# A three-stage attention and MLP kernel: first head pair in an older form, four subtractions on another engine, last accumulator in two halves

## The chip, the cores and the metric

The kernel runs on one core of a Trainium2 chip. The metric is device time in microseconds (us) of one execution. Five engines of the core work side by side and wait for each other through semaphores: PE (TensorE, the matrix unit; PEld is its weight load), DVE (VectorE), ACT (ScalarE), POOL (GpSimd) and SP (SyncE, which here only issues DMAs). Each takes its instructions strictly in the order in which the program wrote them, so an instruction that waits holds up all that stand behind it on that engine.

## The reference

Inputs and outputs are float32. Clustered attention over 2 batches, 8 heads, 768 positions and 64 features (16 clusters per head), then two MLPs over 1536 tokens (512 to 2048 to 512):

```python
q_assign = argmax(q/|q| @ (centroids/|centroids|).T)      # k_assign likewise
scores = (q @ k.T) / 8, -1e9 where q_assign != k_assign
x = softmax(scores) @ v                                   # heads side by side: 1536 x 512
h = x @ moe_w_in;  x = (h * cos(h)) @ moe_w_out
h = x @ moe2_w_in; x = where(h > 0, h, exp(min(h, 0)) - 1) @ moe2_w_out
```

## The kernel before

Every product is made from high and low halves of its float32 operands (a rounded copy and the rest), in three matmuls that add into one accumulator. So each operand costs an engine two instructions: a copy (the high half) and a subtraction (the low half).

**Attention.** The 16 heads form 8 pairs (pp = 0 to 7). A pair is prepared (loads of `nat_k`, `nat_q`, `nat_v`; transposes; high and low halves; norms; similarity to the centroids; cluster masks) while the pair ahead of it runs through its 12 steps `qk`, `rowmax`, `expo`, `turn`, `p_hi`, `p_lo`, with `av` behind every third. Pairs 1 to 7 write their halves to tiles `hi` and `lo` and spread them into the operand stacks `X0k, X1k, T0k, T1k` (and q) by six DMAs per tensor (`stack`, L755 to L760). The first pair has a path of its own without those DMAs: `first_pe` transposes each head, `first_hi`, `first_low` and `first_hi2` write the stacks from PSUM, and its two heads are normed, compared and masked one after the other, with nothing on PE to hide behind. In this kernel its Newton steps for the norms, those of the centroids too (`cen_step`, keys `c`), are POOL instructions (`norm_step`, L656 to L662); low half `X1q` goes to POOL through an extra copy `fraw` (`first_raw`); and squares of its second head are folded once on POOL before DVE sums them (L832).

**MLPs.** Each has three token tiles t of 512 and 16 slices f of 128 hidden columns. Tile t = 0 runs `g1` (12 matmuls into h), `act` (the activation, then its halves `GH` on the engine that table `OWN` names and `GL`) and `g2` (12 matmuls into four accumulators) per slice, while `w_part` rebuilds the weights of that slice from their loaded form (L163, L165, L167), and splits them (high half `slot`, low half L175). Tiles 1 and 2 take the slices in pairs p = 0 to 7 with seven half-sized products per pair (`prod`, L480), `post`, and `act2`, whose last step is the subtraction `GL` at L544, for every pair on POOL. Weights of the second MLP take the places of the first's as its last tile frees them (`load_w`).

**What sets the order.** Tables of numbers (`FIRST`, `PAIR`, `STEP`, `HALF`, `UNIT`, `LAST`, `MLP`, `WINO`, `WB`) give each step a time; the program sorts all steps by it and writes them in that order, which is then the order on every engine and of SP's queue. `OWN` and the `_ON` tables name engines. The last accumulators are copied by ACT (`finish`, L561) and stored through SP (L565).

Of the kernel before, what the change touches and what calls it, by code (L numbers as in the profile page):

```python
# [8 lines left out]
F32 = mybir.dt.float32  # L9
# [6 lines left out]
ALU = mybir.AluOpType  # L16
# [1304 lines left out]
```

## Time and profile before

| | us |
|---|---|
| three timed runs: median (lowest to highest) | 789.33 (786.51 to 790.74) |
| the profiled execution, its own time | 789.13 |
| its span | 787.3 |
| busy in the span: PE / DVE / ACT / POOL | 766.7 / 612.9 / 553.8 / 402.3 |
| first scores matmul of the attention | 19.85 after the span's start |
| boundary of the MLPs (first `g1` of the second) | 518.57 |
| last matmul starts | 783.14 |

The table is read against the first line: 1.83 us of the profiled execution lie outside its span. PE is busy in 97% of the span, so time is found in the few stretches in which it idles or runs at the lower of its two clock levels.

### The profile page before, as it was taken

The numbers are of one execution on the slowest core, as the hardware profiler recorded it, in microseconds if no ns is written. First come the engines' busy times: TensorE is split into PE (matmuls) and PEld (weight loads), VectorE is DVE, ScalarE is ACT, GpSimd is POOL, SyncE is SP. The second block draws the span as 40 slices with busy tenths as digits, with TensorE's granted clock in tenths as the row PEclk, the third lists the DMA queues.
The fourth block names the chain that finished last, engine by engine and source line by source line (L and its number), as shares of the span: only waits on it lengthen the run. The fifth ranks groups of instructions, "written<-read, shape, count | busy, mean of one in ns | idle before, by whom it ended". The sixth has DMA issues, their size and how long they took to land.

```text
span 787.3 us, 13051 instructions
## 1 busy us (share of the span) xinstructions
PE 766.7 (97%) x4579; PEld 686.5 (87%) x4579; DVE 612.9 (78%) x1008; ACT 553.8 (70%) x1035; POOL 402.3 (51%) x472
## 2 busy tenths in 40 slices
PE   6899999999999999999999999989999999999998
PEld 5789999999998878889999899968888999999996
DVE  6789899898899989989998844688978577663442
ACT  5788988989989988867666755766755554654343
POOL 7755866866865732444655422251228666532221
PEclk9899999999999999999999999999999999999999
DMA  5546657647437395011123238882000222223221
GB/s 122 121 98 154 147 117 161 138 104 182 101 87 267 39 374 210 1 40 61 62 81 121 71 113 285 292 275 102 0 1 25 110 81 82 81 95 120 81 80 54
DMA packets 72145, 93.27 MB, mean 118 GB/s; under 512 B 31440, under 2 KB 52432, under 8 KB 72080
## 3 DMA queue, kind: packets, MB, share of 16 engines
q1 hardware_dynamic: 71936, 92.41, 39.4%
q8 instruction: 36, 0.59, 0.3%
q14 instruction: 29, 0.24, 0.1%
q10 hardware_dynamic: 144, 0.03, 0.0%
HBM read 58.75 MB, written 15.78 MB: 95 GB/s over the span
## 4 chain that ended last, share of the span: by engine, by line
PE 91%; ACT 3%; POOL 2%; DVE 1%; DMA 1%; issue 1%; SPq 1%; ACTq 0%; POOLq 0%
PE a L280 32%; PE h L480 20%; PE h L221 11%; PE px L1093 8%; PE pt L1062 8%; PE s L1039 4%; PE s L1042 4%; PE pt_sim L874 2%; PE pt_raw L718 1%; ACT P L1053 1%; POOL GL L544 1%; ACT PH L1076 1%; DMA nat_q<-in_q_dram 1%; DMA X1k<-lo 1%; SPq L607 0%
## 5 line engine op out<-in xcount | busy, mean ns | idle before, releaser
L544 POOL TENSOR_TENSOR GL<-A,GH 128x512 fp32r<-128x512 f32 x64 | 93.3, 1463 | 155.2 <-ACT GH L93 118.4
L280 PE MATMUL a<-GH,slot 128*128 128x512 f32 x384 | 124.7, 393 | 0.0
L280 PE MATMUL a<-slot,GH 128*128 128x512 f32 x384 | 118.4, 389 | 0.0
L1082 DVE TENSOR_TENSOR PL<-pt,PH 128x384 fp32r<-128x384 f32 x192 | 99.0, 547 | 16.5 <-ACT PH L1076 16.5
L1076 ACT ACTIVATE PH<-pt 128x384 fp32r<-128x384 f32 x192 | 85.0, 496 | 18.5 <-PE pt L1062 18.3
L1047 DVE TENSOR_REDUCE m<-s 128x1 f32<-128x768 f32 x96 | 91.0, 948 | 4.2 <-PE s L1042 3.5
L1053 ACT ACTIVATE P<-s,m 128x768 f32<-128x768 f32 x96 | 87.3, 910 | 0.9 <-DVE m L1047 0.6
L280 PEld LDWEIGHTS a<-GH,slot 128*128 128x128 f32 x384 | 72.7, 189 | 14.8
L1062 PE MATMUL pt<-ident,P 128*128 128x128 f32 x576 | 84.2, 280 | 0.0
L221 PE MATMUL h<-XH,slot 128*128 128x512 f32 x256 | 83.7, 391 | 0.0
L280 PEld LDWEIGHTS a<-slot,GH 128*128 128x128 f32 x384 | 71.0, 188 | 14.0
L480 PE MATMUL h<-XH,slot 128*128 128x256 f32 x384 | 81.8, 282 | 0.0
L280 PE MATMUL a<-GL,slot 128*128 128x512 f32 x192 | 75.6, 394 | 3.7 <-POOL GL L544 3.7
L280 PE MATMUL a<-slot,GL 128*128 128x512 f32 x192 | 74.8, 389 | 0.0
L1062 PEld LDWEIGHTS pt<-ident,P 128*128 128x128 f32 x576 | 67.3, 142 | 6.3 <-DVE PL L1082 1.2
L93 ACT ACTIVATE GH<-A 128x512 fp32r<-128x512 f32 x86 | 53.9, 627 | 21.2 <-DVE A L539 9.3
L391 POOL TENSOR_TENSOR X<-slot 128x512 f32<-128x512 f32 x32 | 49.0, 1543 | 37.0 <-DVE sums L434 23.5
L480 PEld LDWEIGHTS h<-XH,slot 128*128 128x128 f32 x384 | 65.0, 190 | 0.7
L502 DVE TENSOR_TENSOR X<-X 128x256 f32<-128x256 f32 x32 | 23.4, 733 | 49.1 <-ACT X L500 48.9
L1093 PE MATMUL px<-PL,V 128*128 128x384 f32 x192 | 57.9, 356 | 0.7
L1093 PE MATMUL px<-PH,V 128*128 128x384 f32 x192 | 58.2, 357 | 0.0
L221 PEld LDWEIGHTS h<-XH,slot 128*128 128x128 f32 x256 | 48.2, 189 | 10.3 <-DVE slot L175 0.3
(197 smaller groups left out, 1958.6 us busy)
## 6 DMA issues: line engine op xcount, KB each, us to landing
raw<-in_moe_w_in_dram SPq DMA_DIRECT2D x32, 512.0 KB, 7.9
raw<-in_moe_w_out_dram SPq DMA_DIRECT2D x32, 512.0 KB, 8.8
sd<-sums SPq DMA_DIRECT2D x32, 384.0 KB, 2.3
sums<-sd SPq DMA_DIRECT2D x32, 384.0 KB, 3.5
nat_k<-in_k_dram SPq DMA_DIRECT2D x16, 192.0 KB, 3.3
nat_q<-in_q_dram SPq DMA_DIRECT2D x16, 192.0 KB, 3.8
nat_v<-in_v_dram SPq DMA_DIRECT2D x8, 384.0 KB, 4.4
xr<-row SPq DMA_DIRECT2D x32, 96.0 KB, 3.5
```

Source lines behind the costliest of these rows:

```text
L93: nc.scalar.activation(out=out, in_=in_, func=AF.Copy)
L221: nc.tensor.matmul(h, lhsT=a[:, kd, :], rhs=b, start=(kd == 0 and i == 0), stop=(kd == NKD - 1 and i == 2))
L280: nc.tensor.matmul(accs[m, t][e], lhsT=a, rhs=b, start=(f == 0 and i == 0), stop=(f == NF - 1 and i == 2))
L391: eng.tensor_tensor(out=u[:, i].rearrange("p e n -> p (e n)").rearrange("p (k f) -> p k f", k=NKD), in0=f32(ih), in1=f32(il), op=ALU.add)
L480: nc.tensor.matmul(o, lhsT=x[:, k], rhs=piece(y, k), start=(k == 0 and n == 0), stop=(k == 1 and n == 2))
L544: eng.tensor_tensor(out=GL, in0=A, in1=f32(GH), op=ALU.subtract)
L1047: nc.vector.tensor_reduce(out=m, in_=st[n]["s"][:, :, 0:HW], axis=AX.XY, op=ALU.max, negate=True)
L1053: nc.scalar.activation(out=P, in_=st[n]["s"][:, :, 0:HW], func=AF.Exp, bias=st[n]["m"], accum_out=den_all[:, u % NDEN, j, r, 0:1])
L1062: nc.tensor.transpose(pt[:, c * 128:(c + 1) * 128], st[n]["P"][:, e, c * 128:(c + 1) * 128], ident)
L1076: nc.scalar.activation(out=ph, in_=pt, func=AF.Copy)
L1082: nc.vector.tensor_tensor(out=pl, in0=pt, in1=f32(ph), op=ALU.subtract)
L1093: nc.tensor.matmul(tx[g][:, 0:HW], lhsT=V2s[pp][:, j, c, :], rhs=halves[g][a][:, c, :], start=(n == 0), stop=(n == 2 * C - 1))
```

## The change

The path of the first pair is put in another form: the centroid's Newton steps become 11 DVE instructions (`norm_steps`), `first_raw` goes and `X1q` is a DVE subtraction from PSUM like the other three, the fold on POOL goes, `sims_scale` and `sims_first` of its second head move to DVE, `T1k` moves to ACT and the copy `X1k` to POOL. The centroids load through SP ahead of everything else, and `nat_v` loads between the heads. `GL` of the last two slice pairs (p = 6, 7) of tile 2 of the first MLP goes to DVE. The last of the four last accumulators is made in two column halves, copied by DVE and ACT and stored through SP and ACT's DMA queue. All tables have new numbers, `OWN` new engines.

```diff
-FIRST = ({'cen_sq': -133.4791, 'first_pe:k': -101.4927, ...
+FIRST = ({'cen_sq': -108.5858, 'first_pe:k': -103.3202, ...
...
-... 'load_w': 10.0054}, ...
+... 'load_w': 7.8176}, ...
+G2_LATE = ((0, 2, 6), (0, 2, 7))
...
-HI2_ON = {('k', 0): 'act', ('k', 1): 'act', ('q', 0): 'act', ('q', 1): 'act'}
+HI2_ON = {('k', 0): 'act', ('k', 1): 'pool', ('q', 0): 'act', ('q', 1): 'act'}
-TH_ON = {('k', 0): 'act', ('k', 1): 'dve', ('q', 0): 'act', ('q', 1): 'act'}
+TH_ON = {('k', 0): 'act', ('k', 1): 'act', ('q', 0): 'act', ('q', 1): 'act'}
...
-            for i, (a, b) in enumerate(prods):
-                nc.tensor.matmul(accs[m, t][e], lhsT=a, rhs=b,
-                                 start=(f == 0 and i == 0), stop=(f == NF - 1 and i == 2))
+            cut = 2 if (m, t, f, e) == (1, NTT - 1, NF - 1, 3) else 1
+            for c in range(cut):
+                cs = slice(c * DM // cut, (c + 1) * DM // cut)
+                for i, (a, b) in enumerate(prods):
+                    nc.tensor.matmul(accs[m, t][e][:, cs], lhsT=a, rhs=b[:, cs],
+                                     start=(f == 0 and i == 0), stop=(f == NF - 1 and c == cut - 1 and i == 2))
...
-            eng = nc.vector if G2_ON[m][e][1] == "dve" else nc.gpsimd
+            eng = nc.vector if G2_ON[m][e][1] == "dve" or (m, t, p) in G2_LATE else nc.gpsimd
             eng.tensor_tensor(out=GL, in0=A, in1=f32(GH), op=ALU.subtract)
...
+            if (t, e) == (NTT - 1, 3):
+                for c in range(2):
+                    cs = slice(c * DM // 2, (c + 1) * DM // 2)
+                    if c == 0:
+                        nc.vector.tensor_copy(o[:, cs], acc[:, cs])
+                        nc.sync.dma_start(out=o_v[b, i][:, cs], in_=o[:, cs])
+                    else:
+                        nc.scalar.activation(out=o[:, cs], in_=acc[:, cs], func=AF.Copy)
+                        nc.scalar.dma_start(out=o_v[b, i][:, cs], in_=o[:, cs])
...
-        nc.scalar.dma_start(out=cen[:, 0, :], in_=centroids.rearrange("h c d -> (h c) d"))
+        nc.sync.dma_start(out=cen[:, 0, :], in_=centroids.rearrange("h c d -> (h c) d"))
         for j in range(2):
             load_nat(0, "k", (j,))
             load_nat(0, "q", (j,))
-        load_nat(0, "v")
+            if j == 0:
+                load_nat(0, "v")
...
+        def norm_steps(key):
+            need(("seed", key))
+            ss, x, y, a = nt[key]
+            for _ in range(3):
+                nc.vector.tensor_tensor(out=a, in0=y, in1=y, op=ALU.mult)
+                nc.vector.scalar_tensor_tensor(out=a, in0=a, scalar=-0.5, in1=x, op0=ALU.mult, op1=ALU.mult)
+                nc.vector.scalar_tensor_tensor(out=y, in0=a, scalar=1.5, in1=y, op0=ALU.add, op1=ALU.mult)
+            nc.vector.tensor_tensor(out=y, in0=y, in1=ss, op=ALU.mult)
+            nc.vector.tensor_scalar_add(y, y, 1e-6)
...
-            if js == (1,):
-                nc.gpsimd.tensor_tensor(out=sq[:, 1, :, 0:D // 2], in0=sq[:, 1, :, 0:D // 2], in1=sq[:, 1, :, D // 2:D],
-                                        op=ALU.add)
...
-            eng = nc.vector if js == (0,) else nc.gpsimd
+            eng = nc.vector if pp == 0 else nc.gpsimd
```

Three places of the new order. The first is PE while the first pair runs its steps: `pt_sim` are the similarities of pair 1, whose operands `X0k` and `X1k` come by DMA; `s` are scores, `pt` turned probabilities. Before:

```order
L1039 MATMUL s<-X0k,X0q 128x384 x2
L1042 MATMUL s<-T0k,T0q 128x384 x2
L874 MATMUL pt_sim<-CC,X0k 128x32 x4
L1062 MATMUL pt<-ident,P 128x128 x6
L874 MATMUL pt_sim<-CC,X0k 128x32 x2
L874 MATMUL pt_sim<-CC,X1k 128x32
L1039 MATMUL s<-X0k,X0q 128x384 x2
```

And now:

```order
L1047 MATMUL s<-X0k,X0q 128x384 x2
L1050 MATMUL s<-T0k,T0q 128x384 x2
L882 MATMUL pt_sim<-CC,X0k 128x32 x2
L882 MATMUL pt_sim<-CC,X1k 128x32 x2
L1070 MATMUL pt<-ident,P 128x128 x6
L882 MATMUL pt_sim<-CC,X0k 128x32
L882 MATMUL pt_sim<-CC,X1k 128x32 x2
```

The first use of `X1k` has moved ahead of six transposes and four of the similarities with `X0k`.

The second is POOL in the same stretch, from the last norm step of the first pair (`ny`) to the first low half `lo` of pair 1. Before:

```order
L662 TENSOR_SCALAR ny<-ny 128x12
L996 TENSOR_SCALAR V_332<-nat_v 128x6x64
L894 TENSOR_TENSOR sm<-sm,nrm 128x2x96
L830 TENSOR_TENSOR sq<-nat_k 128x768
L835 TENSOR_TENSOR sq<-sq 128x12x32
L838 TENSOR_TENSOR sq<-sq 128x12x16
L918 TENSOR_TENSOR sm<-sm,desc 128x2x96
L742 TENSOR_TENSOR lo<-raw,hi 128x384
```

And now:

```order
L688 TENSOR_SCALAR ny<-ny 128x12
L841 TENSOR_TENSOR sq<-nat_k 128x768
L843 TENSOR_TENSOR sq<-sq 128x12x32
L846 TENSOR_TENSOR sq<-sq 128x12x16
L765 TENSOR_TENSOR lo<-raw,hi 128x384
```

Three instructions have left this stretch; the copy to `V` stands ahead of all norm steps now.

The third is DVE at the boundary of the MLPs: `A<-A,R` ends an activation, `GL` is its low half, `u` and `slot` are weights of the second MLP. Before, `GL` was on POOL:

```order
L533 TENSOR_TENSOR A<-A,R 128x512
L202 TENSOR_TENSOR XL<-X,XH 128x512 x2
L165 TENSOR_SCALAR u<-u 128x1024
L533 TENSOR_TENSOR A<-A,R 128x512
L175 TENSOR_TENSOR slot_6728<-guest_6633,slot_6728 128x1024
L167 SCALAR_TENSOR_TENSOR u<-raw_6341,u 128x1024
```

And now:

```order
L537 TENSOR_TENSOR A<-A,R 128x512
L203 TENSOR_TENSOR XL<-X,XH 128x512 x2
L537 TENSOR_TENSOR A<-A,R 128x512
L548 TENSOR_TENSOR GL<-A,GH 128x512
L166 TENSOR_SCALAR u<-u 128x1024
L168 SCALAR_TENSOR_TENSOR u<-raw_6225,u 128x1024
L548 TENSOR_TENSOR GL<-A,GH 128x512
L176 TENSOR_TENSOR slot_6723<-guest_6600,slot_6723 128x1024
```

Both `GL` now stand on DVE, the second behind two weight steps.

## Rows read from the trace of the kernel before

**Rows 1.** The page, part 1: busy time of each engine.

```profile
PE 766.7 (97%) x4579; PEld 686.5 (87%) x4579; DVE 612.9 (78%) x1008; ACT 553.8 (70%) x1035; POOL 402.3 (51%) x472
```

**Rows 2.** Windows: length; busy (instructions) of PE, PEld, DVE, ACT, POOL; PE clock; DMA share; GB/s.

```profile
0.00:50.00 50.00, 39.21 (x211) 34.48 (x212) 36.12 (x77) 32.64 (x64) 32.83 (x106) 0.93 0.47 112
50.00:270.00 220.00, 217.97 (x1495) 204.64 (x1494) 199.89 (x384) 203.64 (x465) 154.19 (x219) 1.00 0.58 138
...
518.00:532.00 14.00, 10.34 (x39) 8.06 (x38) 10.58 (x14) 8.80 (x11) 7.84 (x3) 0.88 0.94 318
```

**Rows 3.** Timeline of PE, first pair: start, length, instruction, [idle before <- releaser].

```profile
18.74 0.82 PE L949 MATMUL pt_mask<-identb,M 128*128 128x128 bf16 x6 [0.71 <-DVE M L940]
...
28.55 0.59 PE L874 MATMUL pt_sim<-CC,X0k 128*128 128x32 f32 x4 [1.31 <-DMA X0k<-lo]
...
31.20 0.25 PE L874 MATMUL pt_sim<-CC,X1k 128*128 128x32 f32 x1 [1.21 <-DMA X1k<-lo]
```

**Rows 4.** Windows around and behind the second wait.

```profile
30.00:40.00 10.00, 8.80 (x43) 8.40 (x43) 6.11 (x12) 6.11 (x13) 5.33 (x17) 0.66 0.65 139
32.00:38.00 6.00, 6.00 (x29) 5.84 (x28) 4.18 (x7) 2.93 (x6) 4.04 (x14) 0.50 0.75 163
```

**Rows 5.** Timeline of POOL, first pair.

```profile
19.98 0.51 POOL L996 TENSOR_SCALAR V<-nat_v 128x384 fp32r<-128x384 f32 x1
20.45 0.52 POOL L894 TENSOR_TENSOR sm<-sm,nrm 128x192 f32<-128x192 f32 x1
...
24.11 0.58 POOL L918 TENSOR_TENSOR sm<-sm,desc 128x192 f32<-128x192 f32 x1
24.65 1.00 POOL L742 TENSOR_TENSOR lo<-raw,hi 128x384 fp32r<-128x384 f32 x1
```

**Rows 6.** Timeline of SP, DMA issues of the first and a later pair.

```profile
25.68 0.51 SPq L756 DMA_DIRECT2D X0k<-lo  x1
...
69.59 1.29 SPq L607 DMA_DIRECT2D nat_q<-in_q_dram  x2
80.50 0.59 SPq L979 DMA_DIRECT2D T0k<-Z  x1
```

**Rows 7.** Timeline of PE at the boundary of the MLPs.

```profile
521.29 0.39 PE L280 MATMUL a<-GH,slot 128*128 128x512 f32 x1
525.34 0.50 PE L280 MATMUL a<-GL,slot 128*128 128x512 f32 x1 [3.66 <-POOL GL L544]
...
530.02 0.63 PE L221 MATMUL h<-XH,slot 128*128 128x512 f32 x2
530.49 0.39 PE L221 MATMUL h<-XL,slot 128*128 128x512 f32 x1
```

**Rows 8.** Timeline of POOL: one subtraction of an earlier pair, and that of the boundary.

```profile
508.10 1.30 POOL L544 TENSOR_TENSOR GL<-A,GH 128x512 fp32r<-128x512 f32 x1 [3.84 <-ACT GH L93]
...
519.71 5.58 POOL L544 TENSOR_TENSOR GL<-A,GH 128x512 fp32r<-128x512 f32 x1 [4.30 <-ACT GH L93]
```

**Rows 9.** Timeline of DVE at the boundary, and a subtraction GL there.

```profile
518.81 1.28 DVE L202 TENSOR_TENSOR XL<-X,XH 128x512 fp32r<-128x512 f32 x2
...
522.35 1.21 DVE L167 SCALAR_TENSOR_TENSOR u<-raw,u 128x1024 uint32<-128x1024 uint32 x1
523.49 0.68 DVE L165 TENSOR_SCALAR u<-u 128x1024 uint32<-128x1024 uint32 x1
...
542.08 0.68 DVE L263 TENSOR_TENSOR GL<-A,GH 128x512 fp32r<-128x512 f32 x1
```

**Rows 10.** Timeline of POOL in the second MLP.

```profile
582.63 3.44 POOL L175 TENSOR_TENSOR slot<-u,slot 128x1024 fp32r<-128x1024 f32 x1 [0.63 <-ACT slot L93]
...
596.25 3.00 POOL L361 TENSOR_TENSOR BX<-X,BX 128x512 fp32r<-128x512 f32 x2
```

**Rows 11.** The end of the program: ACT's last copies; landing of the twelve output stores.

```profile
781.53 2.64 ACT L561 ACTIVATE o<-a 128x512 f32<-128x512 f32 x4 [3.69 <-PE a L280]
...
DMA to landing us min/median/max: 2.0/2.1/4.7
```

More of the change, by code (lines that the diff above doesn't have):

```diff
@@ L28 @@
-STEP = {'qk': -0.7084, 'rowmax': -0.484, 'expo': 0.6444, 'turn:0': 1.5027, 'p_hi:0': 1.7761, 'p_lo:0': 2.025, 'turn:1': 1.6032, 'p_hi:1': 2.0128, 'p_lo:1': 2.2586}
-HALF = {'av:0:0': 6.7513, 'av:0:1': 6.3384, 'av:1:0': 6.9826, 'av:1:1': 4.8875, 'av:2:0': 5.1627, 'av:2:1': 6.3004, 'av:3:0': 4.7675, 'av:3:1': 4.6933, 'av:4:0': 4.8112, 'av:4:1': 4.6976, 'av:5:0': 4.8024, 'av:5:1': 6.8253, 'x_main': 7.2376, 'x_low': 7.0237}
-UNIT = {'den_eps': 2.8361, 'recip': 3.7535, 'recip_rows': 6.6707, 'recip_out': 8.4112, 'x_add': 9.2483, 'x_mul': 17.2906}
@@ new lines @@
+STEP = {'qk': -0.8439, 'rowmax': -0.5989, 'expo': 0.4499, 'turn:0': 1.4222, 'p_hi:0': 1.9292, 'p_lo:0': 2.1434, 'turn:1': 1.4486, 'p_hi:1': 1.9304, 'p_lo:1': 2.2468}
+HALF = {'av:0:0': 6.2719, 'av:0:1': 4.8074, 'av:1:0': 4.7218, 'av:1:1': 4.4542, 'av:2:0': 6.276, 'av:2:1': 4.9696, 'av:3:0': 4.6165, 'av:3:1': 6.4759, 'av:4:0': 4.979, 'av:4:1': 6.5822, 'av:5:0': 5.1983, 'av:5:1': 6.4762, 'x_main': 7.0575, 'x_low': 6.9662}
+UNIT = {'den_eps': 2.7037, 'recip': 3.2698, 'recip_rows': 5.4033, 'recip_out': 8.9866, 'x_add': 8.4622, 'x_mul': 16.7153}
@@ L559, in finish @@
             o = wk.tile([128, DM], F32, tag="AR"[e // 2], name="o")
-            if FIN_ON[m, e] == "act":
-                nc.scalar.activation(out=o, in_=acc, func=AF.Copy)
-            else:
-                nc.vector.tensor_copy(o, acc)
-            b, i = divmod(t * (TT // 128) + e, C)
-            nc.sync.dma_start(out=o_v[b, i], in_=o)
+            b, i = divmod(t * (TT // 128) + e, C)
+            if (t, e) == (NTT - 1, 3):
[7 more added lines that the diff above has]
+                        nc.scalar.dma_start(out=o_v[b, i][:, cs], in_=o[:, cs])
+            else:
+                if FIN_ON[m, e] == "act":
+                    nc.scalar.activation(out=o, in_=acc, func=AF.Copy)
+                else:
+                    nc.vector.tensor_copy(o, acc)
+                nc.sync.dma_start(out=o_v[b, i], in_=o)
         made("finish", m, t, e)
@@ L649, in norm_seed @@
             made("seed", key)
+        def norm_steps(key):
[7 more added lines that the diff above has]
+            nc.vector.tensor_scalar_add(y, y, 1e-6)
+            made("steps", key)
         def norm_step(key, i):
@@ L679, in cen_sq @@
             norm_seed("c", css, "c")
-        def cen_step(i):
-            norm_step("c", i)
         def cen_scale():
@@ L787, in first_hi @@
             made("th", w, j)
-        def first_raw(w, j):
-            raw = raws_sb[0, w, j] = pre.tile([64, 2, HW], F32, tag="fraw", bufs=1, name="fraw")
-            src, sc, *_ = first_parts(w, j)
-            nc.scalar.activation(out=raw, in_=src, func=AF.Copy, scale=sc)
-            made("fraw", w, j)
         def first_low(w, j):
@@ L798, in first_low @@
             src, sc, th, xh, xl = first_parts(w, j)
-            if (w, j) == ("q", 1):
-                need(("fraw", w, j))
-                nc.gpsimd.tensor_tensor(out=xl, in0=raws_sb[0, w, j], in1=f32(th), op=ALU.subtract)
-                made("low", w, j)
-                return
             nc.vector.scalar_tensor_tensor(out=xl, in0=src, scalar=sc, in1=f32(th), op0=ALU.mult, op1=ALU.subtract)
@@ L846, in sum_sq @@
             nc.vector.tensor_reduce(out=sss[pp][:, "kq".index(w), cols(js)],
-                                    in_=sqs[pp, w, js][:, cols(js), :, 0:(D // 2 if js == (1,) else D if pp == 0 or SS_ON[w] == "dve" else D // 4 if SSQ == "quarter" else D // 2)],
+                                    in_=sqs[pp, w, js][:, cols(js), :, 0:(D if pp == 0 or SS_ON[w] == "dve" else D // 4 if SSQ == "quarter" else D // 2)],
                                     axis=AX.X, op=ALU.add)
@@ L916, in sims_first @@
             sm = sims_of(pp, js)
-            eng = nc.vector if js == (0,) else nc.gpsimd
+            eng = nc.vector if pp == 0 else nc.gpsimd
             eng.tensor_tensor(out=sm, in0=sm, in1=desc.unsqueeze(1).unsqueeze(1).to_broadcast(list(sm.shape)),
@@ L1199 @@
                 fn, own = named(name)
-                if fn in (first_pe, first_hi, first_raw, first_low, first_hi2, first_stack):
+                if fn in (first_pe, first_hi, first_low, first_hi2, first_stack):
                     at(time, fn, *own, j)
@@ L1203 @@
                     at(time, fn)
-                elif fn is cen_step:
+                elif fn is norm_steps:
                     at(time, fn, *own)
```

14 lines of the change are left out of this document (7 added, 7 removed).

## The prediction

> **What bounds the kernel now.** I read the busy time by engine first. PE is busy for 766.7 us of the 787.3 us span and the next engine for 613 [rows 1], so PE bounds the kernel, and a change can give time only where PE idles, or where its matmuls run at the lower of its two levels (granted clock 0.50, which is 1.2 GHz).
>
> Then the windows say where the 20.6 idle us lie [rows 2]: 10.8 in the first 50 us (50.00 less 39.21), 2.0 from 50 to 270, 3.7 from 518 to 532. The end adds one more piece: the last matmul is issued at 783.14 (table), and 3.8 us of the span are left behind its 0.39. Together that is 20.3, so the rest of the program has next to none. The change touches the first, the third and the last place.
>
> The timelines then say what ended each wait. In the **head** PE starts the masks of the first pair at 18.74, and once the first scores run it waits twice for pair 1: 1.31 us for `X0k` and 1.21 for `X1k`, both tiles filled by DMA from the low half `lo` [rows 3]. Behind the second wait the clock falls: 0.50 through 32 to 38, and 0.66 in the mean from 30 to 40 [rows 4], so those 10 us did the work of 6.6 and 3.4 were lost. At the **boundary** of the MLPs PE waits 3.66 us in one piece for the `GL` that POOL writes [rows 7]. That instruction took 5.58 us, where the same form took 1.30 earlier [rows 8], and while it ran DVE went from one instruction into the next [rows 9]. Behind this wait the clock falls as well: from 525.34 to 530.02 PE issued 13 matmuls of 512 columns in 4.68 us; at the later pace, two in 0.47 (530.02 to 530.49) [rows 7], they would be 3.06. So 1.6 us more were lost.
>
> The Trainium skill ("TensorE: Matmul & The Clock Gate", Part 1, What's actually happening) says that a clock gate is set by "how busy the PE has been recently". The traces agree: 0.50 stands only behind waits, in both places.
>
> **The head, part by part.** The centroids' Newton steps, `X1q` and the second head's two similarity steps become DVE work, others leave DVE: `T1k` for ACT, `X1k` for POOL. The two heads pass through DVE, ACT and POOL one after the other, so this shortens some links of the chain to 18.74 and lengthens others. The nearest rows are the steps of 0.5 to 0.6 us that changed engines [rows 5]; one such link less or more is the bound, and I take 0 for the time of the mask. It hardly matters: PE stands for 2.52 us later, and an earlier mask only lengthens that wait.
>
> What decides is `lo` of pair 1 on POOL, which starts at 24.65 [rows 5]. In the new order three instructions have left the stretch ahead of it: the copy to `V` (0.51) and the two similarity steps (0.52 and 0.58), 1.6 us together. That is the low bound if only they count. The high one is 3.0, if the `ny` chain ahead also ends earlier because the centroids' steps are no longer on POOL, by two or three such links. I take 2.3. The DMAs are issued about a microsecond behind `lo` (25.68 [rows 6]), so `X1k` arrives near 28.9 instead of 31.20. PE doesn't gain all of it. In the new order the first use of `X1k` stands ahead of six turns and several similarities, which in the trace fill the time between the two waits: 28.55 to 29.99, 1.44 us (the second wait is 1.21 and ends at 31.20 [rows 3]). All of it but two similarities, some 1.1 us, must now follow the wait. Net 2.3 − 1.1 = **1.2 us gained**; bounds 0 (1.6 less 1.1, less one link of 0.5) and 1.9. The clock is the open point: the two short waits become one of about the same sum, so I let it fall as it did and count nothing for it.
>
> `nat_v` between the heads puts one transfer more ahead of the second head's loads. Pair 1's loads go out later too. The later pairs' loads stand further back in SP's queue, but SP issues nothing between 70.88 and 80.50 [rows 6], so they move within a gap. I cost them at 0; if that cover were gone, PE would wait as it does for `X0k`, 1.3 us for each pair. All idle of the seven pairs so far is 2.0 [rows 2].
>
> **The boundary.** Both `GL` of the last pair go to DVE, where that form takes 0.68 instead of 1.30 [rows 9, 8]. DVE ends its two `XL` at 520.09 [rows 9], then ends activation `A` (0.6), and `GL` follows: ready by 521.3. PE wants it at 521.68 (first matmul of the group at 521.29, 0.39 long [rows 7]). The second stands behind `u` (0.68) and `u` (1.21) [rows 9], with 0.6 to 0.7 of its own: ready near 523.8. PE wants it after the 12 matmuls of the first group at 0.23, that is at 524.0 plus one more, 524.2. So both are in time by about 0.4 us and **the wait of 3.66 and the 1.6 of slow clock go: 5.3**. The pair ahead (p = 6) puts two more `GL` on DVE, 1.4 us in all, at a time when POOL does the same in 1.30 undisturbed [rows 8] and PE doesn't wait: 0.
>
> In return POOL and DVE change places in the weights. The low half of slice f = 5 of the second MLP goes to POOL, where this form takes 3.44 [rows 10], behind `GL` (1.30) and the residual steps `BX` (1.50 each [rows 10]). PE comes to that slice eight groups of 2.7 us behind 521.29, near 543; POOL would be done within a microsecond of that. A bound below is 0; a bound above is one instruction held up as the one at the boundary was, by 5.58 − 1.30 = 4.3 [rows 8]. I charge 0.9, nearer to 0 since elsewhere in that MLP POOL's 3.44 costs PE nothing. **Net 4.4 gained**, bounds 1.0 and 5.3.
>
> **The end.** ACT copies each last accumulator of 512 columns in 0.66 (2.64 for four), and the output stores land 2.0 to 4.7 us after their issue [rows 11]. Halves of 256 columns, side by side on two engines and two queues, save a part of 0.66 and no more than half of it is column time: 0.3, and the store has half the bytes. In return the six small matmuls add overhead to PE of the order of 0.1. I take **0.3 gained**, bounds 0.8 and, if the store in ACT's queue lands slower than 2.1, a loss of 0.5.
>
> New numbers for all steps reorder the remaining 700 us, where PE is back to back. No row shows a wait that they free: 0, with the attention's whole idle time as bound either way, say 1.5.
>
> **Sum.** 789.13 (the profiled execution's own time, within 0.2 of the median 789.33) − 1.2 − 4.4 − 0.3 = **783.2 us**.
>
> **Rivals.** *A, the clock doesn't fall in the head.* One wait at another place instead of two 1.2 us apart could leave it at 1.00. Then another 3.4 [rows 4] come back: 779.8. For it: PE is busy without a break until the wait. Against: the sum of waiting is unchanged.
>
> *B, the head gives nothing or loses a little.* POOL's copy `V` now stands ahead of all norm steps and waits for `nat_v`, the steps of two heads behind it; if that load is late, what the three instructions gave is spent. Then 784.4, or 786 if one link of the chain and a wait of 0.5 to 1 come on top.
>
> *C, slower: POOL starves at the opening of the second MLP.* `GL` of f = 0, `BX`, the low half of f = 5 and `GL` of f = 2 stand in one row on POOL, while DVE rebuilds weights back to back. If three of them are held up by 4.3 each [rows 8], that is 12.9; less about 1 of slack, and with 1.6 of slow clock behind the waits, PE loses 13.5 on top of 782.3 (the forecast without its charge of 0.9): 795.8. It decides once DVE leaves no gap of 3 us in this stretch. For it speaks the row of 5.58; against it, 1.30 and 3.44 elsewhere [rows 8, 10].
> The Trainium skill ("SBUF — State Buffer", SBUF: two separate sides) states a rule that speaks for C: VectorE with two SBUF inputs and GpSimd take a shared port pair as an exclusive lock, and the loser waits for a whole instruction. The row of 5.58 beside a busy DVE agrees, with more than one instruction of waiting; by the rule each of POOL's four would pay.
>
> *D, a `GL` is late on DVE.* The margins are 0.4 us. If the copies `GH` on ACT or the weight steps run behind by 1 to 2 us, PE waits that long and the clock may fall again: 785 to 786.5.
>
> **Chances.** Forecast 0.45; A 0.20; B 0.16; C 0.07; D 0.12. A with no charge at the boundary and the upper bounds of head and end gives 779.8 − 0.9 − 0.7 − 0.5, near 777.5; B's 786 with D's 2 us gives 788.0: the range is **777.5 to 788.0** and leaves out C and the tails. A measurement of this kernel tells about 0.5% from no change, 3.95 us, so faster means below 785.4: the forecast, A, and a third of B and D, which with the forecast's own tail taken off is 0.70. Between 785.4 and 793.3: 0.23. Slower: 0.07.
>
> **What would show it.** Right: no wait at the boundary and a granted clock of 1.00 from 518 to 532; POOL's first `lo` near 22.3; one wait of 2 to 2.5 us for `X1k` and a window at 0.50 behind it; about 3.5 us between the last matmul and the end. Wrong: POOL rows of 4 us or more between 525 and 545 with PE waiting for them (C), a `GL` of DVE as releaser of PE (D), a first scores matmul later than 20.5 (B), 1.00 from 30 to 40 (A).

## The result, and the profile after

| | before | the change |
|---|---|---|
| median (lowest to highest), 4 runs each | 789.34 us (786.51 to 790.74) | 779.52 us (778.44 to 782.01) |
| ratio, 95% interval | | 0.9885 [0.9846, 0.9923] |
| profiled execution: its time, its span | 789.13, 787.3 | 782.01, 779.9 |

The change is faster by 9.8 us; forecast were 6.1 (783.2), with a range that holds 779.52. The profiled execution of the change is its slowest of the four, which matters below. Busy time by engine, and windows of it (columns as in [rows 2]):

```profile
PE 764.5 (98%) x4582; PEld 685.5 (88%) x4582; DVE 633.1 (81%) x1027; ACT 548.4 (70%) x1030; POOL 387.5 (50%) x453
```

```profile
0.00:50.00 50.00, 40.41 (x223) 36.16 (x223) 39.55 (x95) 33.72 (x67) 28.72 (x90) 0.80 0.49 113
50.00:270.00 220.00, 218.22 (x1488) 203.67 (x1487) 200.71 (x381) 204.11 (x464) 151.82 (x218) 1.00 0.56 137
...
518.00:532.00 14.00, 14.00 (x63) 11.62 (x62) 13.88 (x18) 10.24 (x14) 1.30 (x1) 1.00 0.99 349
...
532.00:780.00 248.00, 244.07 (x1400) 215.53 (x1399) 172.59 (x236) 128.29 (x217) 103.43 (x71) 1.00 0.19 70
```

Against [rows 2], the boundary (518 to 532) has lost its idle time and runs at 1.00 instead of 0.88. The 3.9 idle us behind 532 are the end of the program. In the first 50 us PE idles 9.6 instead of 10.8, but its clock is worse: 0.80 instead of 0.93.

Timeline of PE in the head, which answers to [rows 3], and of POOL, which answers to [rows 5]:

```profile
17.88 0.82 PE L957 MATMUL pt_mask<-identb,M 128*128 128x128 bf16 x6 [0.74 <-DVE M L948]
...
26.29 0.39 PE L882 MATMUL pt_sim<-CC,X0k 128*128 128x32 f32 x2 [0.50 <-ACT hi L750]
27.66 0.37 PE L882 MATMUL pt_sim<-CC,X1k 128*128 128x32 f32 x2 [0.98 <-DMA X1k<-lo]
```

```profile
17.99 0.20 POOL L688 TENSOR_SCALAR ny<-ny 128x12 f32<-128x12 f32 x1
18.40 1.47 POOL L841 TENSOR_TENSOR sq<-nat_k 128x768 f32<-128x768 f32 x1 [0.22 <-issue]
...
21.61 1.00 POOL L765 TENSOR_TENSOR lo<-raw,hi 128x384 fp32r<-128x384 f32 x1
```

`lo` starts 3.0 us earlier (24.65 before) and `X1k` has landed 3.5 us earlier (31.20 before). The first mask stands at 17.88 instead of 18.74. PE waits 1.5 us for pair 1 (0.50 and 0.98) instead of 2.5.

Timeline of DVE at the boundary, which answers to [rows 9], and PE's matmuls there ([rows 7]):

```profile
518.27 0.69 DVE L548 TENSOR_TENSOR GL<-A,GH 128x512 fp32r<-128x512 f32 x1
518.88 0.69 DVE L166 TENSOR_SCALAR u<-u 128x1024 uint32<-128x1024 uint32 x1
519.60 1.23 DVE L168 SCALAR_TENSOR_TENSOR u<-raw,u 128x1024 uint32<-128x1024 uint32 x1
520.74 0.69 DVE L548 TENSOR_TENSOR GL<-A,GH 128x512 fp32r<-128x512 f32 x1
```

```profile
519.59 0.39 PE L284 MATMUL a<-GL,slot 128*128 128x512 f32 x1
...
522.31 0.39 PE L284 MATMUL a<-GL,slot 128*128 128x512 f32 x1
```

Both `GL` are ready 0.6 and 0.9 us before PE wants them (518.96 and 521.43), about as worked out. From the first `g1` of the second MLP to the start of the last matmul the program took 264.57 us (518.57 to 783.14) and now takes 259.15 (516.64 to 775.79): **5.4 us, the size of the wait and the slow clock at the boundary**. The part ahead of it is only 1.9 shorter in this execution (518.57 to 516.64): 1.1 up to the first `g1` of the first MLP (264.39 to 263.27), and 0.8 in the first MLP.

### The profile page after: what moved, and what is told of

Same layout as the page of the kernel before. It is cut to its first block, busy times and chain, and to the rows that moved or that the text cites. A ratio compares the mean times of both kernels' runs of the same rounds, so it can differ in the third digit from the quotient of the medians.

```text
span 779.9 us, 13072 instructions
## 1 busy us (share of the span) xinstructions
PE 764.5 (98%) x4582; PEld 685.5 (88%) x4582; DVE 633.1 (81%) x1027; ACT 548.4 (70%) x1030; POOL 387.5 (50%) x453
## 4 chain that ended last, share of the span: by engine, by line
PE 91%; DVE 4%; ACT 3%; DMA 1%; issue 1%; SPq 1%; ACTq 0%; DVEq 0%
PE a L284 32%; PE h L484 19%; PE h L222 11%; PE px L1101 8%; PE pt L1070 8%; PE s L1047 4%; PE s L1050 4%; PE pt_sim L882 3%; PE pt_raw L741 1%; DVE PL L1090 1%; DVE m L1055 1%; PE pt_mask L957 1%; ACT PH L1084 1%; ACT P L1061 1%; DMA nat_q<-in_q_dram 0%
## 5 line engine op out<-in xcount | busy, mean ns | idle before, releaser
L548 POOL TENSOR_TENSOR GL<-A,GH 128x512 fp32r<-128x512 f32 x60 | 81.4, 1362 | 150.5 <-ACT GH L94 118.3
L284 PE MATMUL a<-GH,slot 128*128 128x512 f32 x384 | 122.9, 390 | 0.0
L284 PE MATMUL a<-slot,GH 128*128 128x512 f32 (+1 forms) x386 | 118.6, 388 | 0.0
L484 PE MATMUL h<-XH,slot 128*128 128x256 f32 x384 | 79.2, 281 | 0.0
L284 PE MATMUL a<-slot,GL 128*128 128x512 f32 (+1 forms) x193 | 74.9, 388 | 0.0
L506 DVE TENSOR_TENSOR X<-X 128x256 f32<-128x256 f32 x32 | 25.4, 795 | 47.0 <-ACT X L504 47.0
L504 ACT ACTIVATE X<-h 128x512 f32<-128x512 f32 x32 | 19.1, 598 | 54.4 <-PE h L484 54.2
```

Source lines behind the costliest of these rows:

```text
L284: nc.tensor.matmul(accs[m, t][e][:, cs], lhsT=a, rhs=b[:, cs], start=(f == 0 and i == 0), stop=(f == NF - 1 and c == cut - 1 and i == 2))
L484: nc.tensor.matmul(o, lhsT=x[:, k], rhs=piece(y, k), start=(k == 0 and n == 0), stop=(k == 1 and n == 2))
L548: eng.tensor_tensor(out=GL, in0=A, in1=f32(GH), op=ALU.subtract)
```

## The experiments

Three questions were left: does the engine of `GL` free the boundary, where does the rest come from, and what sets the clock in the head. All kernels were timed in five rounds beside before.

### Halves of the change: attn_only and mlp_only

```diff
 # attn_only: the change with MLP, OWN, WINO, WB and the whole last accumulator of before, and
-G2_LATE = ((0, 2, 6), (0, 2, 7))
+G2_LATE = ()
 # mlp_only: before with MLP, OWN, WINO, WB, G2_LATE and the halved last accumulator of the change
```

> The change's attention (its path of the first pair and its numbers for the attention) with the MLP numbers, the POOL subtractions and the whole last accumulator of before. If the two parts add, the boundary wait of 3.7 us on PE stays and only the head gains: first scores matmul near 19.0 instead of 19.85, 1.2 to 2 us less than before, about 787.5, or 784 in executions in which the clock doesn't fall in the head. If the head were the main source of the gain, 781 to 783. A clock that falls in the first 19 us as well would show here, not in the kernel with the MLP part alone.

> The attention of before with the change's MLP numbers, GL of the last two pairs on VectorE and the halved last accumulator. If the boundary is the main source: no PE wait and granted clock 1.00 at the boundary, 5.4 us less than before, 784. If the head carries the gain: 787 or more. The wait for X0k and X1k and the clock at 0.50 behind it stay as they were before.

Measured: attn_only 791.6 (ratio 1.0042 [1.0018, 1.0065]), mlp_only 791.1 (1.0027 [1.0006, 1.0048]), where 787.5 and 784 were expected. Both are slightly slower than before (789.3 beside them), so the halves don't add. Yet each does its own part: attn_only keeps the wait of 3.7 us for `GL` on POOL, mlp_only has no wait at the boundary. What both have more is waits at the opening of the first MLP, where before has no idle time from 275 to 300. From the first `g1` of that MLP to the boundary they take 258.0 and 261.3 us, where before takes 254.2. PE's waits there, of attn_only and then of mlp_only:

```profile
281.33 0.73 PE L222 MATMUL h<-XH,slot 128*128 128x512 f32 x2 [0.96 <-POOL slot L176]
293.45 0.50 PE L222 MATMUL h<-XH,slot 128*128 128x512 f32 x1 [1.19 <-DVE slot L96]
294.71 0.73 PE L222 MATMUL h<-XH,slot 128*128 128x512 f32 x2 [0.53 <-DVE slot L176]
```

```profile
281.77 0.50 PE L284 MATMUL a<-GL,slot 128*128 128x512 f32 x1 [0.84 <-DVE GL L264]
290.59 0.50 PE L222 MATMUL h<-XH,slot 128*128 128x512 f32 x1 [0.53 <-ACT slot L94]
292.50 1.02 PE L222 MATMUL h<-XH,slot 128*128 128x512 f32 x2 [1.18 <-DVE slot L176]
297.77 0.50 PE L284 MATMUL a<-GL,slot 128*128 128x512 f32 x1 [0.89 <-DVE GL L264]
```

The last attention pairs and the first slices of the MLP share DVE, ACT and POOL; that the numbers of the two suit only each other is argued, not shown. The medians of these two runs say nothing on the size of a part; single edits do.

### The boundary: late_only, no_late, row_long

```diff
 # late_only: before, with
+G2_LATE = ((0, 2, 6), (0, 2, 7))
...
-            eng = nc.vector if G2_ON[m][e][1] == "dve" else nc.gpsimd
+            eng = nc.vector if G2_ON[m][e][1] == "dve" or (m, t, p) in G2_LATE else nc.gpsimd
 # no_late: the change, with
-G2_LATE = ((0, 2, 6), (0, 2, 7))
+G2_LATE = ()
 # row_long: before; the last XL of tile 0 of the second MLP is written three times
-        eng.tensor_tensor(out=XL, in0=X[:, kd, t * TT:(t + 1) * TT], in1=f32(XH), op=ALU.subtract)
+        SD["xl", m, t] = SD.get(("xl", m, t), 0) + 1
+        for _ in range(3 if (m, t, SD["xl", m, t]) == (1, 0, NKD) else 1):
+            eng.tensor_tensor(out=XL, in0=X[:, kd, t * TT:(t + 1) * TT], in1=f32(XH), op=ALU.subtract)
```

> Before with one edit: GL of pairs 6 and 7 of the first MLP's last tile on VectorE. If the engine of the four subtractions decides, the 3.7 us wait and the slow clock behind it go, 5.4 us less than before: 784. If the change's new MLP numbers are needed as well (other order of g1 and g2 at the boundary, other engines for the weights), GL is late on VectorE behind weight steps and PE waits for it there 1 to 3 us: 786 to 789.

> The change with all GL back on POOL. If the engine decides: POOL's GL takes 4 to 6 us beside a busy VectorE instead of 1.3, PE waits 3 to 5 us at the boundary and runs at 0.50 behind it: 5 to 7 us more than the change, 785 to 787. If the new order alone had freed the boundary: within 1 us of the change, 779.5.

> Before with one instruction of the boundary written three times (the last XL of the second MLP's first tile; the result is the same): two more VectorE instructions of 0.6 us in the unbroken row beside which POOL's GL took 5.58. If POOL's GL can't run until VectorE's row breaks: GL takes about 6.8, PE's wait for it grows from 3.7 to 4.9, 1.2 us more than before in executions that wait there. If GL is slow for another reason (DMA traffic, ACT), it still ends at about the same distance from its start, 5.6, and the time is that of before.

late_only: 784.08, 0.9953 [0.9931, 0.9975]. One edit gives 5.2 us of median. In its profile the stretch from the boundary to the last matmul is 260.2 us (520.15 to 780.37), 4.3 less than before. Executions with a mean clock of 0.997 or more say the same: 786.4 to 787.1 in before beside it, 782.1 to 782.6 in late_only. PE still waits there for the `GL` of DVE, without a fall of the clock:

```profile
524.20 0.50 PE L281 MATMUL a<-GL,slot 128*128 128x512 f32 x1 [0.75 <-DVE GL L545]
```

The engine is enough for most of the 5.4.

no_late: 781.14, 0.9912 [0.9884, 0.9940], where 785 to 787 was expected. The stretch takes 260.5 us (519.60 to 780.06). So the new order is nearly enough too. DVE, POOL and PE of no_late at the boundary:

```profile
521.84 0.68 DVE L166 TENSOR_SCALAR u<-u 128x1024 uint32<-128x1024 uint32 x1
522.55 2.20 DVE L168 SCALAR_TENSOR_TENSOR u<-raw,u 128x1024 uint32<-128x1024 uint32 x1
```

```profile
521.52 4.39 POOL L548 TENSOR_TENSOR GL<-A,GH 128x512 fp32r<-128x512 f32 x2 [5.49 <-ACT GH L94]
```

```profile
523.72 0.50 PE L284 MATMUL a<-GL,slot 128*128 128x512 f32 x1 [0.63 <-POOL GL L548]
```

The first `GL` starts at 521.52 and PE has it at 523.72. If it ran for the usual 1.3 us, that was from about 522.4 on, when `u` had ended. There DVE's row has a break (522.52 to 522.55), since the next step `u` reads what the one ahead of it wrote; and that step then took 2.20 instead of 1.22. In before two other instructions stand between these two steps:

```profile
520.01 0.68 DVE L165 TENSOR_SCALAR u<-u 128x1024 uint32<-128x1024 uint32 x1
520.62 0.68 DVE L533 TENSOR_TENSOR A<-A,R 128x512 f32<-128x512 f32 x1
521.22 1.21 DVE L175 TENSOR_TENSOR slot<-guest,slot 128x1024 fp32r<-128x1024 f32 x1
```

DVE went on without a break until 524.17, and POOL's `GL`, started at 519.71 during an `XL`, ended at 525.29, 1.1 us behind it [rows 8, 9]. If it ran for 1.3 at the end, it had missed the ends of five DVE instructions in a row.

row_long was meant to make that row longer, and is **faster** than before: 785.95, 0.9962 [0.9948, 0.9976]; the stretch takes 260.8 us (519.96 to 780.80) instead of 264.6. POOL and DVE of row_long:

```profile
521.10 1.53 POOL L546 TENSOR_TENSOR GL<-A,GH 128x512 fp32r<-128x512 f32 x1 [4.31 <-ACT GH L93]
```

```profile
520.20 3.71 DVE L204 TENSOR_TENSOR XL<-X,XH 128x512 fp32r<-128x512 f32 x4
```

The repeated instructions write the same tile, so each waits for the one ahead: two breaks more. `GL` took 1.53 instead of 5.58, and the four `XL` 3.71, about 1.2 more than four times 0.61. PE waits 1.57 us for `XL` in place of 3.66 for `GL`. The expectation was wrong: the length of the row alone doesn't make `GL` wait.

But a break isn't needed either. The second `GL` of row_long started during `slot`, and `u` follows `slot` as closely as one DVE instruction follows another elsewhere. `GL` took 1.46, and `u` 2.32 instead of 1.22:

```profile
525.94 1.46 POOL L546 TENSOR_TENSOR GL<-A,GH 128x512 fp32r<-128x512 f32 x1 [3.31 <-ACT GH L93]
```

```profile
525.03 1.22 DVE L175 TENSOR_TENSOR slot<-guest,slot 128x1024 fp32r<-128x1024 f32 x1
526.17 2.32 DVE L167 SCALAR_TENSOR_TENSOR u<-raw,u 128x1024 uint32<-128x1024 uint32 x1
```

So it is shown that what stands in DVE's row, and where, decides whether `GL` takes 5.58 or 1.5 to 2.2 us. In two cases it got in at a break. Why the `GL` of before missed five ends in a row, where this one got in at the first, is open; a break of known length at a place of choice was not tried.

The Trainium skill ("SBUF — State Buffer", SBUF: two separate sides) has the two engines lock a shared port pair for an instruction, whichever starts first. The stretched DVE rows agree. That a `GL` which has started doesn't get its turn for 4.5 us, through several VectorE instructions, is more than the page states.

### The head: sims_pool and hi2_act

```diff
 # sims_pool: the change, in sims_scale and sims_first
-            eng = nc.vector if pp == 0 else nc.gpsimd
+            eng = nc.vector if js == (0,) else nc.gpsimd
 # hi2_act: the change, with
-HI2_ON = {('k', 0): 'act', ('k', 1): 'pool', ...
+HI2_ON = {('k', 0): 'act', ('k', 1): 'act', ...
```

> The change with sims_scale and sims_first of the first pair's second head back on POOL. By my sum POOL's first lo of pair 1 comes 1.1 us later (near 22.7 instead of 21.6), and PE's wait for X1k grows from 1.0 to about 2: 1 us more in the head. If something else than POOL's queue sets lo (the raw transposes on PE, the hi on ACT), lo and the wait stay within 0.3.

> The change with one edit in the head: the copy X1k back on ACT, out of POOL's row of norm steps, where it takes 0.82. If POOL's row sets when the first lo of pair 1 starts: 0.8 earlier, X1k lands earlier by as much, PE's wait for it (0.5 to 1.0) nearly goes, up to 0.8 us less in the head. If ACT's copy is late there, the similarities with X1k wait and the masks come later: 0 to 1 us more.

sims_pool 780.41 (0.9908 [0.9875, 0.9941]), hi2_act 778.07 (0.9861 [0.9842, 0.9880]). In neither did `X1k` move as much as POOL's row alone would say. Beside a run of the change with the clock at 1.00 (after_rep, below), sims_pool has `lo` 0.6 later (21.91 to 21.31; the second step comes behind it), and `X1k` arrives only 0.18 later (27.59 to 27.41). The head is longer all the same, by 0.8 at the first `g1` of the first MLP (259.59 to 258.82), near the 1 expected: POOL's later steps come later too. Its median is 2.5 above that of after_rep (777.88, timed beside it), since six of its eight executions ran 779.8 to 781.3; why so many is not shown. In hi2_act POOL is done with its row 0.8 earlier, and then stands:

```profile
21.27 1.01 POOL L765 TENSOR_TENSOR lo<-raw,hi 128x384 fp32r<-128x384 f32 x1 [0.72 <-ACT raw L756]
```

SP's issues in hi2_act come from 21.73 on, in after_rep from 21.77:

```profile
21.73 0.54 SPq L778 DMA_DIRECT2D X0k<-hi  x1
22.38 0.53 SPq L779 DMA_DIRECT2D X0k<-lo  x1
22.96 0.59 SPq L780 DMA_DIRECT2D X1k<-hi  x1
23.61 0.59 SPq L781 DMA_DIRECT2D X1k<-lo  x1
```

So in the change ACT's copies `raw` and `hi` set the start of the row of issues, and POOL is no longer the bound. What more POOL gains there is worth nothing; what it loses still costs (sims_pool).

### The clock in the head: after_rep, warm, warm2, late_warm

```diff
 # warm: the change, on PE (spare columns; nothing reads them)
+            for _ in range(8):                      # ahead of the centroids' transpose
+                nc.tensor.transpose(pt[:, 384:512], ident, ident)
+                    for _ in range(8):              # ahead of the first matmul with X1k of pair 1
+                        nc.tensor.transpose(pt[:, 384:512], ident, ident)
 # warm2: warm, and ahead of the first pair's first masks
+                for _ in range(8):
+                    nc.tensor.transpose(pm[:, 768:896], identb, identb)
 # late_warm: late_only with three such groups: centroids, X0k, X1k
```

> The changed kernel itself once more, for the spread of its executions: between 778 and 782.5. If the granted clock in the head falls in some executions and not in others, the short ones carry a mean clock of 0.997 or more and the long ones 0.99 or less, 3 to 4 us apart. If the clock has no part in the spread, time and clock are unrelated.

> The change with sixteen extra 128x128 transposes on PE that fill two of its waits in the head (eight ahead of the centroids' transpose, eight ahead of the first use of X1k); their results are not used. If the waits are what lets the clock fall: 1.00 through the first 50 us in nearly all executions, 2 to 3 us less than the change in the median, 777, and a smaller spread. If the clock falls for other waits too (for the masks, for P), 0.50 still stands in some windows and the time is that of the change, within 1 us. If the fill delays PE: up to 1.8 us more.

> The kernel warm with eight more unused transposes (bf16) ahead of the first pair's masks, in the wait for M that was left there (1.57 us in warm, with 0.50 behind it from about 17 to 23). If that wait lets the clock fall: 1.00 through 0 to 50 us, first scores a few tenths earlier, 777.3 to 777.8. If PE at 0.50 in that stretch only eats its own waits for the vector engines: the clock may rise but the time stays at 777.9 within 0.3.

> The kernel late_only (before with the four GL on VectorE) with three groups of eight unused transposes in PE's waits of the head: ahead of the centroids' transpose and of the first uses of X0k and X1k. late_only ran in two groups of six, 782.1 to 782.6 at a mean clock of 0.999 and 785.6 to 786.4 at 0.993. If the clock in the head is all that parts them: one group near 782.5, none above 784. If something else does: two groups again. If the fill delays PE, one group up to 2 us higher.

| | median | lowest to highest, runs | ratio, 95% interval |
|---|---|---|---|
| after_rep | 777.88 | 777.34 to 782.37, 8 | 0.9906 [0.9872, 0.9939] |
| warm | 777.96 | 777.74 to 778.23, 6 | 0.9889 [0.9852, 0.9926] |
| warm2 | 777.46 | 777.17 to 777.63, 4 | 0.9851 [0.9833, 0.9870] |
| late_warm | 783.14 | 782.65 to 784.18, 6 | 0.9927 [0.9909, 0.9944] |

The change has 12 executions in all: 7 from 777.3 to 778.5 and 5 from 779.7 to 782.4. The profile of after_rep is one of the first kind, that of the change one of the second. Windows, of the change and then of after_rep:

```profile
10.00:20.00 10.00, 8.54 (x42) 7.57 (x42) 8.99 (x23) 4.45 (x9) 7.74 (x28) 0.55 0.01 2
...
30.00:40.00 10.00, 10.00 (x49) 9.46 (x49) 6.08 (x10) 6.63 (x14) 3.11 (x11) 0.58 0.64 119
```

```profile
10.00:20.00 10.00, 8.96 (x42) 8.11 (x43) 8.95 (x24) 4.46 (x8) 7.81 (x27) 1.00 0.01 3
...
30.00:40.00 10.00, 9.47 (x72) 9.08 (x71) 9.22 (x17) 8.65 (x19) 4.69 (x12) 1.00 0.61 115
```

The same kernel does 49 or 72 matmuls between 30 and 40 us, and its span is 779.9 or 775.5. The mean clock of the whole execution doesn't part the two kinds, as it was expected to: four of the seven short ones have 0.990 or 0.991, one of the long ones 0.995. Where the fall lies matters, and that only a profile tells.

With filled waits, warm, warm2 and late_warm have 1.00 from 24 us on in their profiles, and none of their 16 executions is of the long kind. late_only, which is late_warm without the fill, ran at 782.1 to 782.6 or 785.6 to 786.4, six times each; late_warm has one group, up to 784.18, and its fill costs some 0.9 us against the short ones. This speaks for the waits as what lets the clock fall there. It is a matter of counts: the four executions of hi2_act, without fill, are short as well. And not every fall is gone: warm has no execution above 0.996, where 1.00 was expected through the head. The Trainium skill ("TensorE: Matmul & The Clock Gate", Part 1, What's actually happening) has the clock follow "how busy the PE has been recently". The filled kernels agree from 24 us on; why one program falls in some executions only, these runs don't show.

Where the clock falls decides its price. warm2, still at 0.65 in one stretch of the head:

```profile
16.00:24.00 8.00, 7.21 (x39) 6.16 (x40) 7.14 (x14) 5.58 (x11) 7.05 (x13) 0.65 0.18 41
...
28.00:40.00 12.00, 11.47 (x88) 11.06 (x87) 11.06 (x22) 10.61 (x23) 5.91 (x17) 1.00 0.61 123
```

Its profiled span, 775.1, is even below after_rep's 775.5. From 16 to 24 PE waits for masks and probabilities anyway, and slow matmuls use up those waits; hi2_act, at 0.52 there and 1.00 from 24 on, ran 777.85 in that execution. From 28 on PE hardly waits, and there the fall costs about 4 us: the first matmul with `X1k` comes only 0.25 later in the profile of the change than in that of after_rep (27.66 to 27.41), but the first `g1` of the first MLP 4.45 (263.27 to 258.82).

warm2 is the best version measured. Against the short executions of the change it gains next to nothing; none of its four is long.

### The end: end_act

```diff
 # the change, both halves of the last accumulator on ACT
-                    if c == 0:
-                        nc.vector.tensor_copy(o[:, cs], acc[:, cs])
...
+                    nc.scalar.activation(out=o[:, cs], in_=acc[:, cs], func=AF.Copy)
+                    (nc.sync if c == 0 else nc.scalar).dma_start(out=o_v[b, i][:, cs], in_=o[:, cs])
```

> The change with both halves of the last accumulator copied by ACT one after the other (no VectorE), still stored through two queues. If the second half is late only because ACT waits for VectorE's copy of the same bank, the stretch from the last matmul's end to the end of the span, 3.8 us in every kernel so far, becomes 3.6 to 3.7. If the store's landing sets the end: 3.8 again. In the time of the whole neither can be told from the change.

Measured 779.61 (0.9901 [0.9863, 0.9940]). The last matmul of end_act ends at 774.12 and its span at 778.0: 3.9. In the change it is 776.07 to 779.9, 3.8, and in before 783.53 to 787.3, 3.8, all the same within the rounding. In the change the two copies don't run side by side, ACT waits for VectorE:

```profile
776.10 0.42 DVE L569 COPY o<-a 128x256 f32<-128x256 f32 x1 [6.08 <-PE a L284]
```

```profile
776.56 0.38 ACT L572 ACTIVATE o<-a 128x256 f32<-128x256 f32 x1 [0.57 <-DVE o L569]
776.98 0.37 ACTq L573 DMA_DIRECT2D out_dram<-o  x1
```

But end_act, without that wait, issues its last store 0.19 sooner behind the last matmul's start (773.84 to 774.84, where the change has 775.79 to 776.98) and ends no sooner: that store lands 2.1 us after its issue, in the change 1.9. So a quicker copy bought nothing here; what sets the end beyond it is not shown.

## Why the prediction was right, and where it was off

The direction and the place were right: 783.2 forecast, 779.52 measured, inside 777.5 to 788.0. The gain was 9.8 instead of 6.1, and part of the difference is luck: the four executions behind 779.52 are two short and two long ones, so their median lies between the two kinds. By its steps:

- **Boundary, 4.4 forecast, 5.4 measured.** The wait of 3.66 and the slow clock behind it went, as worked out. The charge of 0.9 wasn't paid: in the second MLP POOL's and DVE's rows do lengthen each other, but PE doesn't wait.

```profile
533.89 1.99 POOL L365 TENSOR_TENSOR BX<-X,BX 128x512 fp32r<-128x512 f32 x1 [2.11 <-ACT BX L94]
...
537.55 2.85 POOL L176 TENSOR_TENSOR slot<-u,slot 128x1024 fp32r<-128x1024 f32 x1
540.37 2.28 POOL L264 TENSOR_TENSOR GL<-A,GH 128x512 fp32r<-128x512 f32 x1
```

```profile
538.17 3.31 DVE L168 SCALAR_TENSOR_TENSOR u<-raw,u 128x1024 uint32<-128x1024 uint32 x1
```

POOL's subtractions are held up by up to 1 us and DVE's step by 2.1, not by the 4.3 of rival C. The reason given, POOL beside a busy VectorE, was half right: the order of VectorE's row decides as well, and a new order alone nearly frees the boundary (no_late).
- **Head, 1.2 forecast: the term that was mis-sized.** At a clock of 1.00 the gain is 2.5 to 3, an estimate: the first `g1` of the first MLP comes at 258.82 in after_rep and at 262.20 in late_warm, both at 1.00 through 50 us, 3.4 apart, of which late_warm's fill is up to 0.9. The new order of the attention is in it too. `lo` was put at 22.3 and came at 21.3 to 21.6, past my upper bound for the move in after_rep: besides the three instructions, the last `ny` ends 1.7 to 2.0 us earlier (18.19 and 17.89, against 19.90), because POOL starts the heads' steps earlier (8.71 against 9.60) and `X1q`, 1.81 us in the midst of them, gave way to a copy of 0.82. The prediction had counted those links at 0 to 1.4. It also took 0 for the masks, which came 0.9 to 1.2 earlier, and let the sum of PE's two waits stand, which fell from 2.5 to 1.5 or less.
- **The clock, counted as unchanged.** Both cases came true. In the profiled execution it fell, and the head gained 1.1, near the forecast; 7 of 12 executions ran below 778.5, 1.3 or more under rival A's 779.8, and with the long ones alone the change would stand near 781.7. Rival A's condition, no fall in the head, is seen in the profile of after_rep; four of the other short executions have a mean clock of 0.990 to 0.991, so it fell in them too; in the profile of hi2_act, at 0.990, the fall lay ahead of 24 us. The chance belongs to the execution, and a single profile can't give it. That the shorter waits make the fall rarer isn't shown: a mean clock of 0.997 or more stands in 13 of 55 executions of before and in 3 of 12 of the change.
- **The first MLP, put at 0 with the other reordering, gave 0.8**: from its first `g1` to the boundary before takes 254.2 us and the change 253.4, in both of its profiles. The prediction had found no row with a wait there.
- **End, 0.3 forecast, 0.0 measured**, within a tenth. The second copy waited for the first, and without that wait (end_act) the end came no sooner.
- Rivals B, C and D didn't come: no first scores matmul later than 20.5, no PE wait for POOL in the second MLP, no `GL` late.

Open is a smaller group of before, 9 of those 55 executions below 785.4. By their times they might not wait at the boundary, but no profile caught one.

## What to carry to other kernels

When an instruction on GpSimd takes several times its usual time beside VectorE, look at which VectorE instructions it stands beside, and try both remedies: move the GpSimd instruction to another engine, or change the order of VectorE's row. Either was worth about 4 us here. Before timing small edits, look at how executions of one kernel spread and at the clock of each: a fall behind a wait can be worth more than the edit. Unused matmuls in the waits are worth a try: with them no long execution was seen. A clock that fell where the engine waits anyway cost next to nothing.

## What was not expected of the hardware

Two more VectorE instructions in the busiest stretch made the kernel 3.7 us faster (789.65 to 785.95 beside each other): with them GpSimd's `GL` took 1.53 instead of 5.58. And the granted clock of one and the same program differs from execution to execution: 0.58 or 1.00 from 30 to 40 us, 4.4 us of span.
